# Linear attention with a routed expert layer: the first key group's maxima and exponentials unit by unit, its keys in three transfers, and one product on zeros less

## Chip, cores, metric

One core of a Trainium2 chip. The metric is the device time of one execution of the whole program in microseconds, as the median of several runs. A profiled execution gives the trace from which the rows below are taken.

## What is computed

```python
def phi(x):                                   # random-feature map, M = 128 features
    proj = einsum('bhsd,md->bhsm', x, omega)
    h = proj - sum(x * x, axis=-1, keepdims=True) / 2
    h = h - max(h, axis=-1, keepdims=True)
    return exp(h) / sqrt(m)
q_p, k_p = phi(q * scale), phi(k * scale)     # batch 4, heads 8, sequence 576, head size 64
kv = einsum('bhsm,bhsd->bhmd', k_p, v)
z = sum(k_p, axis=2)
attn = einsum('bhsm,bhmd->bhsd', q_p, kv) / (einsum('bhsm,bhm->bhs', q_p, z)[..., None] + 1e-6)
x = attn as [2304, 512]
# then: logits = x @ w_gate, each row goes to the expert of its largest logit (8 experts, capacity 576),
# out = gate weight * (relu(x @ w1[e]) @ w2[e])
```

## The kernel before

The kernel writes out the order of every engine's instructions by hand; what each engine waits for follows from the tiles that an instruction reads and writes. Its time falls into a key stage (to about 48 us), a query stage with the routing (to about 123 us) and the expert stage.

The keys come as 8 chunks (4 batches with 2 halves of the heads each), each 128 x 1152 numbers: 9 units of 128 columns. The loop over `n` takes the 72 units in 18 groups of `KG` = 4. Turn `n` does this:

- `project` (line 147): for each of the four units two products, `om_s` (the scaled features) with the upper and the lower 64 rows of the keys, into two banks `pjk`, four units side by side in each bank. Turns `n` and `n + 2` use the same two banks, so group 2's products overwrite what group 0 left. A product in this number format stands as two records (passes) in the trace, so a group has 16 passes.
- `kv_acc` (line 200): the sums of group `n - 2`, exponentials times values, 32 records, tile `kacc`.
- the maxima over 128 features (VectorE) and the exponentials (ScalarE) of group `n`. For the first bank, one reduction over all four units (line 153) and four exponentials with the negated maximum as bias (line 531); for the second bank, one reduction, one subtraction of the maximum over all four units on VectorE (line 534) and one exponential over all of it (line 535).

On TensorE the order is thus: products of groups 0, 1 and 2, sums of group 0, products of group 3, sums of group 1, and so on.

Ahead of the loop TensorE multiplies zeros (`warm`, line 244), `WARM` = 3 times, each as two passes. The first chunk's keys (`kraw`) come in pieces whose borders are `FIRST_CUTS`; with 0, 128, 384, 768, 1152 group 0 (units 0 to 3) needs the first three pieces, group 1 (units 4 to 7) the third and fourth, and group 2 unit 8 of the fourth and three units of the next chunk. All of these transfers are issued by SP, one after another, with the first values (`v`) behind the second piece.

Of the kernel before, what the change touches and what calls it, by code (L numbers as in the profile page):

```python
# [13 lines left out]
AF = mybir.ActivationFunctionType  # L14
ALU = mybir.AluOpType
AX = mybir.AxisListType
# [3 lines left out]
B, H, S, D, M = 4, 8, 576, 64, 128  # L20
# [2 lines left out]
NT = N // 128  # L23
ROW = 73
SLOTS = 576
FIRST_CUTS = [0, 128, 384, 768, 1152]
SUB = 128
NSUB = 5
REST = SLOTS - 4 * SUB
# [6 lines left out]
NJ = 11  # L36
EPS = 1e-6 * M
BIG = 1048576.0
WARM = 3

HI_AT = ({0: ((1, 2),), 1: ((1, 3),), 2: ((2, 0),), 3: ((2, 1),), 4: ((2, 2),), 5: ((2, 3),)}, {0: ((2, 0),), 1: ((2, 1),), 3: ((2, 2),), 4: ((2, 3),)})
LO_AT = ({0: ((1, 2),), 1: ((1, 3),), 3: ((2, 0),), 4: ((2, 1),), 5: ((2, 2),), 6: ((2, 3),)}, {1: ((2, 0),), 2: ((2, 1),), 5: ((2, 2),), 6: ((2, 3),)})
# [8 lines left out]
def attention_moe(ctx, tc, kT, qT, va, om, wg, w1, w2, cap, ident, tri, desc, lst, tab0, out):  # L51
    nc = tc.nc
# [12 lines left out]
    def bank(i, name):  # L65
        return ps.tile([128, 512], F32, tag=f"b{i}", name=name, bufs=1)

    def pair(name):
        return ps.tile([128, 1024], F32, tag="a2", name=name, bufs=1)
# [55 lines left out]
    def start(gen):  # L125
        tasks.append([gen, None])

    def run(at=None, times=1, most=99):
        for _ in range(times):
            for task in list(tasks):  # L130
                if task[1] is None or (task[1] == at and most > 0):
                    most -= task[1] is not None
                    try:
                        task[1] = next(task[0])
                    except StopIteration:
                        tasks.remove(task)
# [6 lines left out]
    def project(parts, banks):  # L143
        for k, x in enumerate(parts):
            for i in range(2):
                rows = slice(64 * i, 64 * i + 64)
                nc.tensor.matmul(banks[i][:, k * M : (k + 1) * M], x[rows, :], om_s[rows, :], start=True, stop=True)  # L147

    def units(x):
        return x.rearrange("p (a m) -> p a m", m=M)  # L150

    def maxima(mx, i, src):
        nc.vector.tensor_reduce(mx[:, 4 * i : 4 * i + 4], src, op=ALU.max, axis=AX.X, negate=True)  # L153

    def spread(mx, i):
        return mx[:, 4 * i : 4 * i + 4].unsqueeze(2).to_broadcast([128, 4, M])
# [6 lines left out]
    def load_q(c):  # L163
        n0, n1 = QB[c] * 128, QB[c + 1] * 128
        raw = qp.tile([128, NP, QT * 128], F32, tag="qraw", name=f"qraw{c}")
        nc.sync.dma_start(raw[:, :, 0 : n1 - n0], qT[:, :, n0:n1])
        qc[c] = raw
# [8 lines left out]
    def load_k(b, g):  # L176
# [3 lines left out]
        if b == 0 and g == 0:  # L180
            for i, (c0, c1) in enumerate(zip(FIRST_CUTS, FIRST_CUTS[1:])):
                nc.sync.dma_start(raw[:, c0:c1], kT[b, :, g * W + c0 : g * W + c1])
# [12 lines left out]
    def kv_acc(b, g, t, ex, k, acc):  # L195
        v = chunks[b, g][1]
        a, z, o = (t, t + 1, 0) if t < 4 else ((4, 6, 0) if t == 4 else (t + 1, t + 2, VW))
        for i in range(2):
            for f in (0, 64):
                nc.tensor.matmul(  # L200
                    acc[f : f + 64, i * 2 * VW + o : i * 2 * VW + o + (z - a) * VW],
                    ex[:, 4 * i + k, f : f + 64],
                    v[:, i, a * VW : z * VW],
                    start=(t == 0 and i == 0),
                    stop=(t == 8),
                    skip_group_check=True,
                )
# [34 lines left out]
    wps = bank(SM, "wps")  # L242
    for _ in range(WARM):
        nc.tensor.matmul(wps[:, 0:256], warm[:, 0:128], warm, start=True, stop=True)
# [209 lines left out]
    def numer(t, qpT, acc):  # L454
        for p in range(NP):
            for i in range(2):
                for r in (0, 64):
                    nc.tensor.matmul(  # L458
                        acc[r : r + 64, i * 512 + p * ROW : i * 512 + (p + 1) * ROW],
                        qpT[:, 4 * i + p, r : r + 64],  # L460
                        kv_sb[(t * 128 + r) // S][:, 2 * p + i, :],
                        start=(p == 0),
                        stop=(p == NP - 1),
                        skip_group_check=True,
                    )
# [23 lines left out]
    NK = len(KU) // KG  # L489
    ex_l, d_l, qT_l, acc_l = {}, {}, {}, {}  # L490

    for n in range(NK + NT + 3):
        kn, t = n, n - NK
        mx = small.tile([128, H], F32, tag="mx", name=f"mx{n}", bufs=4) if n < NK + NT else None

        if n < NK:
            pj = [bank(2 * (n % 2) + i, f"pjk{n}{i}") for i in range(2)]
            project([chunks[b, g][0][:, u * 128 : (u + 1) * 128] for b, g, u in KU[KG * n : KG * n + KG]], pj)
        elif t < NT:
            pj = [bank((2 * t + i) % 3, f"pjq{n}{i}") for i in range(2)]  # L500
            c = max(i for i in range(len(QB) - 1) if QB[i] <= t)
            o = (t - QB[c]) * 128
            project([qc[c][:, p, o : o + 128] for p in range(NP)], pj)
        run("T")

        if 0 <= t - 2 < NT:
            d = d_l.pop(t - 2)
            trs = [bank(3 + i, f"qtr{n}{i}") for i in range(2)]
            for u in range(H):
                nc.tensor.transpose(trs[u // 4][:, (u % 4) * M : (u % 4 + 1) * M], d[:, u, :], id_sb)  # L510
        run()

        if 0 <= n - 2 < NK:
            ex = ex_l.pop(n - 2)
            for k, (b, g, u) in enumerate(KU[KG * (n - 2) : KG * (n - 1)]):
                if u == 0:
                    acc_l[0] = bank(4, f"kacc{b}{g}") if g == 0 else pair(f"kacc{b}{g}")
                kv_acc(b, g, u, ex, k, acc_l[0])
                if u == 8:
                    start(kv_gate(b, g, acc_l[0]))  # L520
        elif 0 <= t - 3 < NT:
            acc_l[0] = pair(f"qacc{t}")
            numer(t - 3, qT_l.pop(t - 3), acc_l[0])
        run("N")

        if n < NK:
            ex = kp.tile([128, H, M], F32, tag="ex", name=f"ex{n}", bufs=3)
            maxima(mx, 0, units(pj[0]))
            run()
            for k in range(4):  # L530
                nc.scalar.activation(ex[:, k, :], pj[0][:, k * M : (k + 1) * M], AF.Exp, bias=mx[:, k : k + 1], scale=1.0)  # L531
            maxima(mx, 1, units(pj[1]))
            run()
            nc.vector.tensor_tensor(ex[:, 4:8, :], units(pj[1]), spread(mx, 1), op=ALU.add)
            nc.scalar.activation(ex[:, 4:8, :], ex[:, 4:8, :], AF.Exp)
            ex_l[n] = ex
            run()
        else:
            if t < NT:
                d = qp.tile([128, H, M], F32, tag="d", name=f"d{t}", bufs=3)  # L540
                nc.scalar.copy(d[:, 0:4, :], units(pj[0]))
                maxima(mx, 1, units(pj[1]))
                run()
                maxima(mx, 0, d[:, 0:4, :])
                nc.gpsimd.tensor_tensor(d[:, 0:4, :], d[:, 0:4, :], spread(mx, 0), op=ALU.add)  # L545
                d_l[t] = d
            run("P", times=2, most=2)
            if 0 <= t - 2 < NT:
                qpT = qp.tile([128, H, M], F32, tag="qpT", name=f"qpT{t}", bufs=2)
                for i in range(2):  # L550
                    nc.scalar.activation(qpT[:, 4 * i : 4 * i + 4, :], units(trs[i]), AF.Exp)
                qT_l[t - 2] = qpT
                run()
            if t < NT:
                for k in range(4):
                    nc.scalar.activation(
                        d[:, 4 + k, :], pj[1][:, k * M : (k + 1) * M], AF.Identity, bias=mx[:, 4 + k : 5 + k], scale=1.0
                    )
                run()
            if 0 <= t - 3 < NT:  # L560
                normalise(t - 3, acc_l[0])
                if t - 3 in GROUPS:
                    start(route(*GROUPS[t - 3]))
                if t == 3:
                    start(first_item())
            run(times=3)
        run("E")

        if n == NK + 1:
            kstack.close()  # L570
            open_experts()
        if n < NK:

            for k in range(KB, 2 * B):
                if (9 * (k - KB) + 8) // KG + 2 == n:
                    load_k(k // 2, k % 2)
            if n == 3:
                start(setup())
            if n in (NK - 4, NK - 2):
                load_q(0 if n == NK - 4 else 1)  # L580
        elif t < NT and t - QB[c] == 2 and c + 2 < len(QB) - 1:
            load_q(c + 2)
# [265 lines left out]
```

## Time and profile before

| | |
|---|---|
| median of 3 runs | 296.16 us (295.9 to 296.26) |
| the profiled execution's own time | 297.4 us |
| its span, first to last instruction | 295.3 us |
| TensorE busy | 277.4 us, 94% |
| VectorE busy | 162.8 us, 55% |
| ScalarE busy | 152.9 us, 52% |
| mean granted clock of TensorE | 0.978 |

Shares over the whole span hide that the stages have different limits; the change lies in the first ten microseconds, which are 3% of the span, and what they are worth is read from when TensorE's unbroken row of work begins. In the rows, PE is TensorE, PEld its weight loads, DVE VectorE, ACT ScalarE, POOL GpSimd, SP the engine that issues most transfers (SPq its queue). A time in a timeline is counted from the span's start.

### The profile page before, as it was taken

The numbers are of one execution on the slowest core, as the hardware profiler recorded it, in microseconds if no ns is written. First come the engines' busy times: TensorE is split into PE (matmuls) and PEld (weight loads), VectorE is DVE, ScalarE is ACT, GpSimd is POOL, SyncE is SP. The second block draws the span as 40 slices with busy tenths as digits, with TensorE's granted clock in tenths as the row PEclk, the third lists the DMA queues.
The fourth block names the chain that finished last, engine by engine and source line by source line (L and its number), as shares of the span: only waits on it lengthen the run. The fifth ranks groups of instructions, "written<-read, shape, count | busy, mean of one in ns | idle before, by whom it ended". The sixth has DMA issues, their size and how long they took to land.

```text
span 295.3 us, 7405 instructions
## 1 busy us (share of the span) xinstructions
PE 277.4 (94%) x2958; PEld 240.7 (81%) x2958; DVE 162.8 (55%) x357; ACT 152.9 (52%) x371; POOL 75.2 (25%) x78
## 2 busy tenths in 40 slices
PE   7999999999999969799999999999999999999960
PEld 5898898889988958799957879996888899868850
DVE  1998788578887896576834332543333152532220
ACT  1887788868888745155416324543541345342410
POOL 1000000422674315750718100700121162011120
PEclk9999999999999987999999999999999999999995
DMA  6989730328667702286029914910811097064010
GB/s 204 395 310 364 244 139 4 99 66 287 232 201 261 293 36 73 86 271 238 2 60 372 372 52 111 332 42 4 269 65 73 36 295 152 0 178 165 37 54 28
DMA packets 29504, 48.01 MB, mean 163 GB/s; under 512 B 4835, under 2 KB 17507, under 8 KB 29444
## 3 DMA queue, kind: packets, MB, share of 16 engines
q1 hardware_dynamic: 26900, 41.45, 41.9%
q0 software_dynamic: 2416, 5.92, 6.3%
q8 instruction: 25, 0.41, 0.6%
q14 instruction: 19, 0.16, 0.2%
q10 hardware_dynamic: 144, 0.07, 0.1%
HBM read 35.61 MB, written 12.10 MB: 162 GB/s over the span
## 4 chain that ended last, share of the span: by engine, by line
PE 88%; DVE 4%; issue 2%; DMA 1%; ACT 1%; SPq 0%; POOL 0%
PE hi L676 9%; PE hi L678 9%; PE hi L677 9%; PE qacc L458 7%; PE yi L693 7%; PE kacc L200 7%; PE yi L694 7%; PE yi L695 7%; PE pjq L147 6%; PE pjk L147 6%; PE qtr L510 5%; PE xtri L328 3%; DVE xr L475 1%; DMA kraw<-kT 1%; PE yi0r L705 1%
## 5 line engine op out<-in xcount | busy, mean ns | idle before, releaser
L676 PE MATMUL hi<-xhi,w1hi 128*128 128x288 f32 x192 | 57.0, 297 | 0.0
L678 PE MATMUL hi<-xlo,w1hi 128*128 128x288 f32 x192 | 56.6, 295 | 0.0
L677 PE MATMUL hi<-xhi,w1lo 128*128 128x288 f32 x192 | 56.5, 294 | 0.0
L681 ACT ACTIVATE hhii<-hi 128x288 fp32r<-128x288 f32 (+1 forms) x48 | 18.5, 385 | 46.6 <-PE hi L678 45.4
L545 POOL TENSOR_TENSOR d<-d,mx 128x512 f32<-128x512 f32 x18 | 18.7, 1038 | 86.1 <-DVE mx L153 79.6
L693 PE MATMUL yi<-w2hi,hhii 128*128 128x512 f32 x96 | 39.0, 406 | 0.0
L684 DVE SCALAR_TENSOR_TENSOR hloi<-hi,hhii 128x288 fp32r<-128x288 f32 (+1 forms) x48 | 20.3, 423 | 33.3 <-ACT hfi L683 21.8
L694 PE MATMUL yi<-w2hi,hloi 128*128 128x512 f32 x96 | 38.0, 396 | 0.0
L695 PE MATMUL yi<-w2lo,hhii 128*128 128x512 f32 x96 | 37.9, 395 | 0.0
L334 DVE TENSOR_TENSOR xlo<-xtri,xhi 128x512 fp32r<-128x512 f32 (+1 forms) x20 | 12.5, 635 | 45.5 <-ACT xhi L332 45.5
L676 PEld LDWEIGHTS hi<-xhi,w1hi 128*128 128x128 f32 x192 | 36.0, 188 | 0.2
L677 PEld LDWEIGHTS hi<-xhi,w1lo 128*128 128x128 f32 x192 | 36.0, 188 | 0.0
L678 PEld LDWEIGHTS hi<-xlo,w1hi 128*128 128x128 f32 x192 | 36.0, 188 | 0.0
L98 POOL DMA_INDIRECT out<-ysi,idx x10 | 9.8, 981 | 73.6 <-ACT ysi L727 45.1
L314 POOL DMA_INDIRECT xg<-x_d,idx x15 | 19.0, 1264 | 35.8 <-PE hi L678 22.4
L153 DVE TENSOR_REDUCE mx<-pjk 128x4 f32<-128x512 f32 x36 | 23.1, 684 | 6.4 <-PE pjk L147 6.1
L458 PE MATMUL qacc<-kv_sb,qpT 128*64 128x73 f32 x576 | 23.4, 235 | 2.6 <-DVE xr L475 2.6
L458 PEld LDWEIGHTS qacc<-kv_sb,qpT 128*64 128x64 f32 x576 | 20.8, 141 | 5.8 <-issue 4.0
L531 ACT ACTIVATE ex<-pjk,mx 128x128 f32<-128x128 f32 x72 | 20.5, 368 | 7.0 <-DVE mx L153 6.5
L98 POOL DMA_INDIRECT tab_d<-pay,slot x18 | 19.3, 1070 | 15.8 <-DVE slot L399 10.6
L147 PE MATMUL pjk<-om_s,kraw 64*128 64x128 f32 x288 | 22.1, 292 | 1.1 <-ACT ex L531 0.6
L200 PE MATMUL kacc<-v,ex 128*64 128x65 f32 (+1 forms) x576 | 22.6, 230 | 0.2 <-issue 0.2
(126 smaller groups left out, 472.9 us busy)
## 6 DMA issues: line engine op xcount, KB each, us to landing
w1raw<-w SPq DMA_DIRECT2D x16, 512.0 KB, 5.9
w2raw<-w SPq DMA_DIRECT2D x16, 512.0 KB, 6.4
qraw<-qT SPq DMA_DIRECT2D x6, 768.0 KB, 6.2
x_d<-xr SPq DMA_DIRECT2D x18, 256.0 KB, 2.9
v<-va SPq DMA_DIRECT2D x7, 650.0 KB, 7.5
kraw<-kT SPq DMA_DIRECT2D x7, 576.0 KB, 7.1
out<-zero_sb SPq DMA_DIRECT2D x4, 768.0 KB, 7.9
out<-ysi SPq DMA_DIRECT2D x4, 256.0 KB, 4.6
```

The lines of the kernel that those rows point to most:

```text
L98: ins = nc.gpsimd.indirect_dma_start(out=dst, out_offset=bass.IndirectOffsetOnAxis(ap=index, axis=0), in_=src, in_offset=None, bounds_chec ...
L147: nc.tensor.matmul(banks[i][:, k * M : (k + 1) * M], x[rows, :], om_s[rows, :], start=True, stop=True)
L153: nc.vector.tensor_reduce(mx[:, 4 * i : 4 * i + 4], src, op=ALU.max, axis=AX.X, negate=True)
L200: nc.tensor.matmul(acc[f : f + 64, i * 2 * VW + o : i * 2 * VW + o + (z - a) * VW], ex[:, 4 * i + k, f : f + 64], v[:, i, a * VW : z * VW] ...
L458: nc.tensor.matmul(acc[r : r + 64, i * 512 + p * ROW : i * 512 + (p + 1) * ROW], qpT[:, 4 * i + p, r : r + 64], kv_sb[(t * 128 + r) // S][ ...
L531: nc.scalar.activation(ex[:, k, :], pj[0][:, k * M : (k + 1) * M], AF.Exp, bias=mx[:, k : k + 1], scale=1.0)
L676: nc.tensor.matmul(pt, whi_[:, k, fs], xhi[:, k, sl], start=(k == 0), stop=False)
L677: nc.tensor.matmul(pt, wlo_[:, k, fs], xhi[:, k, sl], start=False, stop=False)
L678: nc.tensor.matmul(pt, whi_[:, k, fs], xlo[:, k, sl], start=False, stop=(k == 3))
L693: nc.tensor.matmul(pt, hhi[:, f, sl], w2hi, start=(f == 0), stop=False)
L694: nc.tensor.matmul(pt, hlo[:, f, sl], w2hi, start=False, stop=False)
L695: nc.tensor.matmul(pt, hhi[:, f, sl], w2lo, start=False, stop=(f == 7))
```

## The change

Three edits. `FIRST_CUTS` becomes 0, 128, 512, 1152: group 0 needs two pieces, group 1 the third alone. `WARM` becomes 2. In turn 0 alone, the maxima and exponentials go unit by unit, the two banks taking turns: for each unit one reduction over 128 columns and one exponential with its result as bias; the subtraction on VectorE and the exponential over 512 columns are gone for this group.

```diff
-FIRST_CUTS = [0, 128, 384, 768, 1152]
+FIRST_CUTS = [0, 128, 512, 1152]
...
-WARM = 3
+WARM = 2
...
         if n < NK:
             ex = kp.tile([128, H, M], F32, tag="ex", name=f"ex{n}", bufs=3)
+        if n == 0:
+
+            for k in range(4):
+                for i in range(2):
+                    u, src = 4 * i + k, pj[i][:, k * M : (k + 1) * M]
+                    nc.vector.tensor_reduce(mx[:, u : u + 1], src, op=ALU.max, axis=AX.X, negate=True)
+                    nc.scalar.activation(ex[:, u, :], src, AF.Exp, bias=mx[:, u : u + 1], scale=1.0)
+            ex_l[n] = ex
+        elif n < NK:
             maxima(mx, 0, units(pj[0]))
```

VectorE's queue from the scaling of the features on, before (`mx` holds the maxima, `pjk_133` and `pjk_134` are group 0's two banks, `pjk_153` and `pjk_154` group 1's; in brackets the semaphores that an instruction waits for):

```order
L250 TENSOR_SCALAR om_s<-om_sb 128x128 [waits DMAHW0_49]
L153 TENSOR_REDUCE mx_132<-pjk_133 128x4 [waits PE_49]
L153 TENSOR_REDUCE mx_132<-pjk_134 128x4 [waits PE_49]
L534 TENSOR_TENSOR ex_143<-pjk_134,mx_132 128x512 [waits DVE_49]
L153 TENSOR_REDUCE mx_152<-pjk_153 128x4 [waits PE_49]
```

The same place of the change, where the banks of group 0 are `pjk_131` and `pjk_132`:

```order
L250 TENSOR_SCALAR om_s<-om_sb 128x128 [waits DMAHW0_49]
L533 TENSOR_REDUCE mx_130<-pjk_131 128x1 [waits PE_49]
L533 TENSOR_REDUCE mx_130<-pjk_132 128x1 [waits PE_49]
L533 TENSOR_REDUCE mx_130<-pjk_131 128x1 [waits Activation_49]
L533 TENSOR_REDUCE mx_130<-pjk_132 128x1 [waits Activation_49]
L533 TENSOR_REDUCE mx_130<-pjk_131 128x1 [waits Activation_49]
L533 TENSOR_REDUCE mx_130<-pjk_132 128x1 [waits Activation_49]
L533 TENSOR_REDUCE mx_130<-pjk_131 128x1 [waits Activation_49]
L533 TENSOR_REDUCE mx_130<-pjk_132 128x1 [waits Activation_49]
L153 TENSOR_REDUCE mx_158<-pjk_159 128x4 [waits PE_49]
```

Three instructions have become eight, and from the third on each waits for ScalarE, namely for the exponential that read the same bank before it.

TensorE's queue around the first two groups, before (`kraw_100` is the first chunk, `kraw_113` the second):

```order
L147 MATMUL pjk_133<-om_s,kraw_100 128x128 [waits DMAHW1_49,DVE_49]
...
L147 MATMUL pjk_133<-om_s,kraw_100 128x128 [waits DMAHW2_49]
...
L147 MATMUL pjk_133<-om_s,kraw_100 128x128 [waits DMAHW4_49]
...
L147 MATMUL pjk_153<-om_s,kraw_100 128x128 [waits DMAHW5_49]
...
L147 MATMUL pjk_173<-om_s,kraw_100 128x128 [waits DVE_49,Activation_49]
L147 MATMUL pjk_174<-om_s,kraw_100 128x128 [waits DVE_49,PE_49]
L147 MATMUL pjk_173<-om_s,kraw_113 128x128 [waits DMAHW6_49]
```

And of the change, where the second chunk is `kraw_111`:

```order
L147 MATMUL pjk_131<-om_s,kraw_100 128x128 [waits DMAHW1_49,DVE_49]
...
L147 MATMUL pjk_131<-om_s,kraw_100 128x128 [waits DMAHW2_49]
...
L147 MATMUL pjk_159<-om_s,kraw_100 128x128 [waits DMAHW4_49]
...
L147 MATMUL pjk_179<-om_s,kraw_100 128x128 [waits Activation_49]
L147 MATMUL pjk_180<-om_s,kraw_100 128x128 [waits Activation_49]
L147 MATMUL pjk_179<-om_s,kraw_111 128x128 [waits DMAHW5_49]
```

The wait inside group 0 for a third piece is gone, group 1 waits once, ahead of its first unit, and group 2 waits for ScalarE alone to free both banks.

SP's queue loses one transfer and changes two (before with -, the change with +):

```order
 L182 DMA kraw_100<-kT 128x128
-L182 DMA kraw_100<-kT 128x256
+L182 DMA kraw_100<-kT 128x384
 L184 DMA v_101<-va 128x2x260
-L182 DMA kraw_100<-kT 128x384 x2
-L187 DMA kraw_113<-kT 128x1152
+L182 DMA kraw_100<-kT 128x640
+L187 DMA kraw_111<-kT 128x1152
 L185 DMA v_101<-va 128x2x390
```

The second chunk's keys and all later transfers move up by one issue.

## Rows read from the trace of the kernel before

**Rows 1.** Busy time by stretch: length, then each engine, granted clock, DMA share, GB/s:

```profile
0.00:8.47 8.47, 6.17 (x38) 4.48 (x38) 2.38 (x5) 2.42 (x5) 0.95 (x7) 1.00 0.73 223
8.47:50.00 41.53, 41.30 (x840) 36.90 (x840) 36.39 (x68) 34.05 (x98) 0.00 (x0) 1.00 0.69 250
```

**Rows 2.** What TensorE waited for, 8.4 to 50 us: total, times, longest:

```profile
PE pjk L147 <- ACT ex L531: 0.6, 1, 0.6
```

**Rows 3.** The chain that ended last: shares, then 0 to 13 us (start, length, what):

```profile
PE 88%; DVE 4%; issue 2%; DMA 1%; ACT 1%; SPq 0%; POOL 0%
...
2.15 3.84 DMA kraw<-kT
...
6.57 0.69 DVE mx L153
...
7.28 1.15 ACT ex L531 x4
...
8.47 1.37 PE pjk L147 x16
9.85 1.08 PE kacc L200 x32
```

**Rows 4.** Timeline of VectorE, 4 to 11 us: start, length, instructions:

```profile
6.55 1.29 DVE L153 TENSOR_REDUCE mx<-pjk 128x4 f32<-128x512 f32 x2 [3.43 <-PE pjk L147]
7.88 0.69 DVE L534 TENSOR_TENSOR ex<-pjk,mx 128x512 f32<-128x512 f32 x1
```

**Rows 5.** Timeline of TensorE, 0 to 12 us (second row: 1.7 to 2.6):

```profile
1.18 2.93 PE L244 MATMUL wps<-warm 128*128 128x256 f32 x6 [1.18 <-DVE warm L241]
...
1.18 1.65 PE L244 MATMUL wps<-warm 128*128 128x256 f32 x3 [1.18 <-DVE warm L241]
...
4.04 1.65 PE L147 MATMUL pjk<-om_s,kraw 64*128 64x128 f32 x12
6.03 0.94 PE L147 MATMUL pjk<-om_s,kraw 64*128 64x128 f32 x12 [0.34 <-DMA kraw<-kT]
...
10.86 1.16 PE L147 MATMUL pjk<-om_s,kraw 64*128 64x128 f32 x16
```

**Rows 6.** Timelines of SP's queue and of VectorE, 0 to 5 us:

```profile
0.73 0.90 SPq L182 DMA_DIRECT2D kraw<-kT  x2
...
2.15 0.94 SPq L182 DMA_DIRECT2D kraw<-kT  x2
3.13 0.43 SPq L187 DMA_DIRECT2D kraw<-kT  x1
...
2.90 0.23 DVE L250 TENSOR_SCALAR om_s<-om_sb 128x128 f32<-128x128 f32 x1 [1.77 <-DMA om_sb<-om]
```

**Rows 7.** us from issue to landing: second piece, fourth piece, second chunk:

```profile
kraw<-kT SPq DMA_DIRECT2D x1, 128.0 KB, 2.2
...
kraw<-kT SPq DMA_DIRECT2D x1, 192.0 KB, 4.4
...
kraw<-kT SPq DMA_DIRECT2D x1, 576.0 KB, 5.6
```

**Rows 8.** TensorE's timeline around 110 us, and that stretch as in rows 1:

```profile
108.92 0.24 PE L374 MATMUL posr<-cum,ones_b 128*128 128x96 bf16 x1 [2.43 <-DVE cum L362]
...
109.21 2.08 PE L147 MATMUL pjq<-om_s,qraw 64*128 64x128 f32 x16
...
113.11 2.19 PE L458 MATMUL qacc<-kv_sb,qpT 128*64 128x73 f32 x32
...
108.30:115.10 6.80, 6.17 (x58) 5.44 (x57) 5.73 (x20) 2.81 (x7) 2.37 (x3) 0.50 0.11 41
```

**Rows 9.** Prices by line and form: count, busy us, mean ns of one:

```profile
L153 DVE TENSOR_REDUCE mx<-pjk 128x4 f32<-128x512 f32 x36 | 23.1, 684 | 6.4 <-PE pjk L147 6.1
...
L348 DVE TENSOR_REDUCE mxr<-lg 128x12 f32<-128x96 f32 x1 | 0.3, 253 | 0.0
...
L531 ACT ACTIVATE ex<-pjk,mx 128x128 f32<-128x128 f32 x72 | 20.5, 368 | 7.0 <-DVE mx L153 6.5
```

## The prediction

> **What bounds the kernel now.** I read the table of stretches first, then the chain of work that ended last, then the timelines of the first 11 us, since all three edits lie there. The stretches show TensorE busy for 41.30 of 41.53 us from 8.47 to 50, while VectorE and ScalarE have 5 to 7 us to spare; ahead of 8.47 it is busy for 6.17 of 8.47 [rows 1]. From 8.4 to 50 us its list of waits has one of note, 0.6 us, which is the one that ends at 8.47 [rows 2]. So from 8.47 on the key stage is a row of products, and what happens ahead of it is worth what it moves that start. The later stages follow TensorE as well: 88% of the whole chain is its work [rows 3], and the waits on VectorE in it come behind products of the same stage and move with them.
>
> The chain says what sets that start: a piece of keys lands at 2.15 + 3.84 = 5.99, the last passes of group 0 follow, VectorE's first maxima from 6.57, ScalarE's four exponentials from 7.28 to 8.43, and at 8.47 group 2's products, which overwrite group 0's banks [rows 3]. VectorE leaves the second bank at 7.88 + 0.69 = 8.57 [rows 4]; group 0's sums (from 9.85) come only behind group 2's products. Three things therefore must happen earlier if the kernel is to gain: the two banks of group 0 must come free, the keys of group 2 must be there, and group 1's products must be done.
>
> **The end of the warm products.** Each product stands as two passes. The three on zeros run from 1.18 to 4.11, three passes end at 2.83 and six at 4.11, so a pass is (4.11 - 2.83) / 3 = 0.427 us [rows 5]. The first key product starts at 4.04, 0.07 before the last record ends. With four passes the records end at 4.11 - 0.85 = 3.26, and the first key product can start at 3.19. Its other inputs are there: om_s is written by 2.90 + 0.23 = 3.13, and the first two pieces of keys had landed by 1.2 + 2.2 = 3.4 in their old size (SP issues the two from 0.73 in 0.90 us) [rows 6, 7]. The second piece grows from 128 to 192 KB. That costs between nothing and 64 KB at the 223 GB/s of the stretch to 8.47, 0.29 us [rows 1]; I take the latter, 3.7. Unit 0's passes occupy TensorE from 3.19 for about 0.6 us, so unit 1 is not held.
>
> **Group 0's products.** In the old order two pieces (3.4 and 5.99) had to land before the fourth unit. Now all four units run at one go. Twelve such passes took 1.65 us from 4.04 and 0.94 from 6.03 [rows 5], so the start ran at the slower pace, and sixteen passes at that pace stand at 109.21, where the granted clock was 0.50: 2.08 us [rows 8]. They end at 3.19 + 2.08 = 5.27, and VectorE starts about 0.03 later, at 5.30, against 6.55 [rows 4]: **1.25 us earlier**.
>
> **Maxima and exponentials unit by unit.** What VectorE does is two reductions over 512 (1.29 us) and an addition (0.69); it becomes eight reductions over 128. No such reduction stands in the trace. It is bounded by 0.253 (over 96) and 0.684 (over 512), which differ by 1.04 ns an element, so 0.253 + 32 x 1.04 = 0.286 us [rows 9]. ScalarE's four small exponentials and one of 512 become eight small ones, 0.368 each [rows 9].
>
> They do not overlap freely. The order shows that from the third on each reduction waits for ScalarE: it is the exponential that read the same bank just before. So in one bank the two engines take turns. A turn is 0.286 + 0.02 to ScalarE (the maximum ends at 6.57 + 0.69 = 7.26, the exponential starts at 7.28) + 0.368 + 0.04 back (as from ScalarE's 8.43 to TensorE's 8.47) = 0.715 us [rows 3]. Four turns less the last way back are 2.83 us for the first bank. The second trails by the spacing of two exponentials, (1.15 - 0.368) / 3 = 0.26 us [rows 3]: 3.09. Before, the banks came free 8.43 - 6.55 = 1.88 and 7.88 + 0.69 - 6.55 = 2.02 us after the start. **The new way takes about 1.0 us longer**, and gives back most of the 1.25: 5.30 + 2.83 = 8.13 against 8.43, and 8.39 against 8.57. With 0.04 to TensorE, group 2 starts at 8.17 and its second bank at 8.43: **-0.2 us**.
>
> The Trainium skill bears on this ("PSUM — Partial Sum Buffer", section "PSUM bank collisions raise a hardware error"): two engines may not touch one bank in the same partitions at once, reads by ScalarE and VectorE included. If that were not so, eight exponentials spaced by 0.26 behind the first maximum would end at 5.30 + 0.31 + 7 x 0.26 + 0.37 = 7.80, by which the banks would no longer be what group 2 waits for. No run here shows the two reading one bank together; the waits in the order show that this program does not try.
>
> **Group 1.** It needs the third piece, 320 KB, where it needed two pieces of 192 that landed at 5.99 and, issued with 0.47 us of SP for each, at 2.62 + 4.4 = 7.0 [rows 3, 6, 7]. The bytes ahead are the same, so I bound the landing by these two and take 6.9. Sixteen passes at full pace took 1.16 us [rows 5], with the last one starting some 0.27 before the end: TensorE is free for group 2 at 7.8 (at the late bound 8.0), still ahead of 8.17. VectorE is through with group 0 about 0.4 ahead of ScalarE, near 8.0, and takes up group 1 then; nothing waits for that.
>
> **Group 2's keys.** Its units 1 to 3 come from the next load, issued at 3.13 and landed 5.6 us later, 8.7 [rows 6, 7]. That is already within 0.2 us of being what holds group 2. One issue fewer moves it up by at most 0.47; if the engines' bytes alone set it, by nothing. With no move group 2 gains 0.03; with 0.2 or more it gains the full 0.2. I take **-0.15 us**. Later loads each wait for an older transfer, now one place earlier in the list; TensorE waited for none of them [rows 2].
>
> **Sum.** The profiled execution's own time is 297.4 us, 2.1 over its span of 295.3; the median of the plain runs is 296.16. -0.15 on either gives a span of 295.15 and a median of **296.0 us**. A measurement of this kernel can tell about 0.2%, 0.6 us, from no change, so this counts as no change.
>
> **Rivals.**
>
> *The clock comes later (slower).* By the two rows of twelve passes TensorE went from the lower level, 1.2 GHz, to 2.4 GHz between 5.7 and 6.3 us, although the granted clock is listed as 1.00 from the start [rows 1, 5]. Ahead of that it had worked from 1.18 with one pause of 0.34 us. Now it stops at about 5.1 and waits for the third piece until 6.9. If it stays at the lower level, group 1 takes 2.08 instead of 1.16, so group 2 starts at about 8.8, not 8.2, +0.35 on the 8.47 of before; if the clock stays low through group 2 and group 0's sums as well (2.08 instead of 1.16, and twice 1.08 [rows 3, 5, 8]), +0.35 + 0.92 + 1.08 = +2.35. Middle: +1.3, 297.5. For it speaks that at 109.21 work went on for some 6 us at 0.50 after a pause of 2.43 us [rows 8]; against it that ahead of 5.1 TensorE would have worked nearly 4 us with hardly a break. It decides when the clock is still low at 8.2. The page "TensorE: Matmul & The Clock Gate", section "What's actually happening", of the Trainium skill has the throttled state as the default, which activity releases; the trace agrees as far as these rows go, and by it an idle stretch moved into the start-up is a risk. Chance 0.26, of which two thirds pass 0.6 us.
>
> *The turns cost more.* If each hand-over took 0.1 more, seven of them move group 2 by +0.7 - 0.2 = +0.5: 296.7. The rows give 0.02 to 0.05 everywhere, so 0.06.
>
> *The turns cost less and the keys come with the issue (faster).* With 0.2 for a reduction and 0.3 for an exponential a turn is 0.56 and the banks are free at 7.8; keys at 8.7 - 0.47 = 8.2 leave -0.5 to -0.6: 295.6. Chance 0.12.
>
> *The pause in the middle falls elsewhere (faster).* At 108.3 the clock fell to 0.50, after TensorE had waited from 106.5 for VectorE's routing, and came back at 115.1; the work from 109.21 to 113.11 + 2.19 = 115.30 took 6.1 us, half of it for the halved clock [rows 8]. Any move of the work can change how much of it falls into the slow stretch; half of those 3 us saved would be -1.5: 294.6. Nothing in the rows says that 0.15 us suffices: 0.12.
>
> **How the numbers follow.** No change of note is left with 0.44, its own range 295.6 to 296.6. Faster by over 0.6 us: the middle pause 0.12, nearly half of the quick turns, and some of the main case's edge: 0.20. Slower: two thirds of the late clock, half of the costly turns, a little edge: 0.25. The rest, 0.55, is within 0.2%. The range of 294.9 to 297.4 leaves a tenth on each side.
>
> **What would show it.** Group 0's first maximum at 5.3 +-0.15, the last exponential of the turns ending at 8.4, group 2's first product at 8.2, and group 1's sixteen passes in 1.16 us. I am wrong if these still take 2.08, if group 2 starts later than 8.5, or if the stretch of low clock behind 105 us is of another length.

## The result and the profile after

The changed kernel is slower: 298.09 us (median of 6 runs, 297.73 to 298.46) against 296.21 (295.67 to 297.27), a ratio of 1.0061 [1.0042, 1.008], +1.9 us where 296.0 was forecast. Its profiled execution took 298.25 us over a span of 296.1.

Busy time by stretch of the changed kernel (columns as in [rows 1]):

```profile
0.00:8.47 8.47, 5.08 (x32) 3.76 (x34) 2.64 (x10) 3.55 (x9) 0.95 (x7) 1.00 0.76 250
8.47:50.00 41.53, 41.16 (x816) 36.83 (x816) 34.91 (x65) 32.30 (x94) 0.00 (x0) 0.96 0.68 244
5.60:7.70 2.10, 0.00 (x0) 0.00 (x0) 1.56 (x6) 1.60 (x6) 0.00 (x0) 1.00 0.98 331
9.10:12.50 3.40, 3.40 (x47) 3.12 (x44) 3.33 (x6) 2.65 (x9) 0.00 (x0) 0.50 1.04 403
12.50:50.00 37.50, 37.13 (x766) 33.13 (x764) 31.42 (x60) 29.42 (x85) 0.00 (x0) 1.00 0.65 227
```

Against [rows 1], TensorE's granted clock from 8.47 to 50 is no longer 1.00 but 0.96, and it does 24 records fewer in that stretch (816, not 840) though it is busy nearly all of it. The whole loss of clock lies between 9.1 and 12.5, at 0.50, which is the lower of its two levels, 1.2 GHz. Ahead of it stands a stretch of 2.1 us with no work of TensorE at all, while the DMA engines are busy for 0.98 of the time.

TensorE's timeline of the changed kernel, 0 to 14 us (the products split by group):

```profile
1.19 2.07 PE L244 MATMUL wps<-warm 128*128 128x256 f32 x4 [1.19 <-DVE warm L241]
3.20 2.35 PE L147 MATMUL pjk<-om_s,kraw 64*128 64x128 f32 x16
7.75 1.16 PE L147 MATMUL pjk<-om_s,kraw 64*128 64x128 f32 x16 [2.20 <-DMA kraw<-kT]
8.74 2.06 PE L147 MATMUL pjk<-om_s,kraw 64*128 64x128 f32 x16
10.74 1.96 PE L200 MATMUL kacc<-v,ex 128*64 128x65 f32 x32
12.62 1.16 PE L147 MATMUL pjk<-om_s,kraw 64*128 64x128 f32 x16
```

Group 0's sums in the same view of the kernel before:

```profile
9.77 1.15 PE L200 MATMUL kacc<-v,ex 128*64 128x65 f32 x32
```

Group 0 starts 0.84 earlier than before, as meant. Then TensorE waits 2.20 us for the third piece of keys. Group 1 runs at full pace (16 passes in 1.16); group 2 begins at 8.74, 0.27 later than before; its products take 2.00 to the next row's start and group 0's sums 1.88, where before they took 9.77 - 8.47 = 1.30 and 10.86 - 9.77 = 1.09 [rows 3, 5]. Group 3 begins at 12.62, not 10.86: 0.27 + 0.70 + 0.79 = **1.76 us late**, of which 1.49 is the halved clock.

VectorE's and ScalarE's timelines, then the groups by line and form, of the changed kernel:

```profile
5.58 0.49 DVE L533 TENSOR_REDUCE mx<-pjk 128x1 f32<-128x128 f32 x2 [2.45 <-PE pjk L147]
...
6.30 0.55 DVE L533 TENSOR_REDUCE mx<-pjk 128x1 f32<-128x128 f32 x2 [0.23 <-ACT ex L534]
...
5.90 2.80 ACT L534 ACTIVATE ex<-pjk,mx 128x128 f32<-128x128 f32 x8 [3.45 <-DVE mx L533]
...
L533 DVE TENSOR_REDUCE mx<-pjk 128x1 f32<-128x128 f32 x8 | 2.1, 290 | 3.0 <-PE pjk L147 2.4 <-ACT ex L534 0.6
...
L534 ACT ACTIVATE ex<-pjk,mx 128x128 f32<-128x128 f32 x8 | 2.5, 364 | 3.8 <-DVE mx L533 3.5
```

The turns begin at 5.58, and their last exponential ends at 5.90 + 2.80 = 8.70.

Where the 1.76 go later, the timeline of the changed kernel from 108 us and the middle stretch of low clock:

```profile
110.60 0.20 PE L374 MATMUL posr<-cum,ones_b 128*128 128x96 bf16 x1 [2.43 <-DVE cum L362]
...
123.60 0.40 PE L685 MATMUL hi<-xhi,w1hi 128*128 128x288 f32 x1
...
111.50:114.90 3.40, 3.40 (x30) 2.85 (x28) 3.30 (x12) 1.80 (x4) 0.64 (x1) 0.50 0.22 82
```

The first expert product in the trace of before:

```profile
123.14 0.40 PE L676 MATMUL hi<-xhi,w1hi 128*128 128x288 f32 x1
```

The routing's product stands at 110.60, not 108.92 [rows 8]: 1.68 later, so the start's loss has come through the whole key stage. The clock falls here for 3.4 us, not 6.8, and from this product to the first expert product it is 13.00 us; in the trace of before that product stands at 123.14, 14.22 behind. So the two profiled spans differ by only 0.8 us. That is because the one of before was 297.4, 1.2 over its own median; the plain runs give the change's price.

### The profile page after: what moved, and what is told of

Its sections match the earlier page's. It is cut to its first block, busy times and chain, and to the rows that moved or that the text cites. A ratio compares the mean times of both kernels' runs of the same rounds, so it can differ in the third digit from the quotient of the medians.

```text
span 296.1 us, 7406 instructions
## 1 busy us (share of the span) xinstructions
PE 276.7 (93%) x2956; PEld 240.2 (81%) x2956; DVE 162.7 (55%) x362; ACT 153.6 (52%) x374; POOL 76.4 (26%) x78
## 5 line engine op out<-in xcount | busy, mean ns | idle before, releaser
L334 DVE TENSOR_TENSOR xlo<-xtri,xhi 128x512 fp32r<-128x512 f32 (+1 forms) x20 | 12.5, 634 | 45.5 <-ACT xhi L332 45.5
L314 POOL DMA_INDIRECT xg<-x_d,idx x15 | 19.7, 1313 | 36.5 <-DMA idx<-tab_d 26.4
L458 PE MATMUL qacc<-kv_sb,qpT 128*64 128x73 f32 x576 | 22.8, 231 | 2.6 <-DVE xr L475 2.6
L147 PE MATMUL pjk<-om_s,kraw 64*128 64x128 f32 x288 | 22.8, 301 | 2.2 <-DMA kraw<-kT 2.2
L458 PEld LDWEIGHTS qacc<-kv_sb,qpT 128*64 128x64 f32 x576 | 20.2, 138 | 5.8 <-issue 4.0
L153 DVE TENSOR_REDUCE mx<-pjk 128x4 f32<-128x512 f32 x34 | 21.9, 684 | 4.8 <-PE pjk L147 4.4
L147 PEld LDWEIGHTS pjk<-om_s,kraw 64*128 64x128 f32 x288 | 19.1, 200 | 4.6 <-DMA kraw<-kT 2.7
```

The source lines that it names most:

```text
L458: nc.tensor.matmul(acc[r : r + 64, i * 512 + p * ROW : i * 512 + (p + 1) * ROW], qpT[:, 4 * i + p, r : r + 64], kv_sb[(t * 128 + r) // S][ ...
```

## Experiments

All ratios are to the kernel before, run beside it on the same chip, with a 95% interval; 12 runs each (4 in one case, 11 in another). They are not the quotients of the medians, and where the two differ the text says which it uses. "Filling" means products on zeros into a bank that nobody reads, behind group 0's products; "mid filling" is the same during the routing's wait at 106.5 us. Each kernel does all the work of the reference.

### Is it the clock, the keys or the turns?

Filling the pause with four products (the kernel is otherwise the changed one):

```diff
         project(...)
+        if n == 0:
+            for _ in range(4):
+                nc.tensor.matmul(wps[:, 0:256], warm[:, 0:128], warm, start=True, stop=True)
```

> The changed kernel with four more products on zeros behind group 0's products, where TensorE waits for the third piece of keys (5.5 to 7.75 us). Clock theory (the pause makes the clock fall at about 9 us, and group 2's products and group 0's sums then run at half pace): the clock stays up, group 3's products start near 10.9 instead of 12.62, and the time is 296.2 +-0.5, about 1.9 below the changed kernel. Keys or turns theory (the late third piece or the alternation of maxima and exponentials delays the work itself): the fill changes nothing, 298.1, or costs a little more.

297.35 us, 1.0031 [1.0011, 1.0051]. TensorE's timeline from 5.3 us, and the stretch that was low:

```profile
5.35 2.42 PE L501 MATMUL wps<-warm 128*128 128x256 f32 x8
7.70 2.34 PE L147 MATMUL pjk<-om_s,kraw 64*128 64x128 f32 x32
9.97 1.15 PE L200 MATMUL kacc<-v,ex 128*64 128x65 f32 x32
11.05 1.16 PE L147 MATMUL pjk<-om_s,kraw 64*128 64x128 f32 x16
...
9.10:12.50 3.40, 3.40 (x67) 3.09 (x68) 3.33 (x6) 2.70 (x9) 0.00 (x0) 1.00 1.03 400
```

The piece still lands at about 7.7 and the turns are as before, but the clock holds at 1.00, 67 records fit where there were 47, and group 3 begins at 11.05, 0.19 behind the kernel before. So of the 1.76, 1.57 hang on the pause in this pair of traces. The runs won back only half of the 0.61%, 0.30 +-0.28 by the two intervals, for a reason that this trace does not show in the start; it has the long low stretch (6.8 us) in the middle.

The three edits undone one at a time:

```diff
+WARM = 3                                 # e2
...
+FIRST_CUTS = [0, 128, 384, 768, 1152]    # e3
...
-        if n == 0:
+        if n == -1:                       # e4: the old maxima
```

> The changed kernel with the third warm product put back. Clock theory: group 0's products end 0.85 us later, near 6.4, the pause shrinks from 2.2 to about 1.4 us, and most of the loss goes: 296.2 to 297. Keys or turns theory: the later start of group 0 only adds, 298.1 to 298.9.

298.15 us, 1.0049 [1.0024, 1.0075]. TensorE's timeline, 8 to 11 us:

```profile
8.80 2.33 PE L147 MATMUL pjk<-om_s,kraw 64*128 64x128 f32 x16 [1.12 <-ACT ex L534]
```

The piece was there at 6.52, and the pause moved behind group 1: 1.12 us for the turns' exponentials, again followed by half pace; group 3 at 12.67. Not every execution pays: three of the 12 took 295.93 to 296.11 us, at a mean granted clock of 0.983 to 0.984, the other nine 297.64 to 299.55, eight of them at 0.976 to 0.978.

> The changed kernel with the old pieces of keys (borders 128, 384, 768). Clock theory: TensorE works again at 6 us, when the third piece lands, no pause is over 1 us, and the time is that of before, 296.2 +-0.5. Keys theory: 296.2 as well. Turns theory: the alternation starts at 6.6 and holds group 2 until 9.5, 297.2 to 298.

299.22 us (4 runs), 1.0108 [1.0094, 1.0123], the slowest of all. TensorE's timeline, 9 to 16 us:

```profile
9.36 2.33 PE L147 MATMUL pjk<-om_s,kraw 64*128 64x128 f32 x16 [1.25 <-ACT ex L534]
11.62 2.00 PE L200 MATMUL kacc<-v,ex 128*64 128x65 f32 x32
13.55 2.08 PE L147 MATMUL pjk<-om_s,kraw 64*128 64x128 f32 x16
```

Without the new cuts the wait for the turns is 1.25 us, and TensorE, which had not yet been at full pace, stays at half pace past group 3. Beside the new maxima the new cuts were the part that helped, not the part that hurt (1.0042 to 1.008 with them, 1.0094 to 1.0123 without); the theory that the 320 KB piece is the cause falls.

> The changed kernel with group 0's maxima and exponentials in the old way (one reduction for each bank); cuts and warm products as changed. Clock theory: the pause is the same, 298.1 +-0.4. Turns theory: the banks come free 1 us earlier, 296.5 to 297. Keys theory: 298.1.

296.67 us, 1.0015 [0.9991, 1.0039]: with the old maxima alone back, no loss is seen. TensorE's one pause of note in the start is 0.76 us (for the second piece); in this trace too it works at half pace until about 10.3, and group 3 begins at 11.71. I had held that the pause for the third piece would stay and cost as much, and that fell. In this execution the third piece was there when group 1 came to it, so the trace does not show the old maxima beside a late piece; that they cost no more than 0.39% over before is seen in the 12 runs.

### The same with the middle held

On this chip every kernel, that of before too (310.83), took some 14 us more. In the traces it lies in waits of TensorE behind 116 us, the longest for VectorE; ratios on one chip are hardly touched by that.

```diff
         pos_b = bank(SM, ...)
+        if a == 0:
+            for _ in range(5):
+                nc.tensor.matmul(pos_b[:, 256:512], warm[:, 0:128], warm, start=True, stop=True)
```

These three lines alone, in the kernel before:

> The kernel before with five products on zeros ahead of the routing's first product, into columns of its bank that nobody reads, so that TensorE works through the pause from 106.3 to 108.9 us. Clock theory: the clock doesn't fall there, the 6 us of work at half pace take 3, and the time falls by 1.5 to 3 us to 293.5 to 295, with less spread between runs. If the low clock in the middle costs nothing (the routing's chain on VectorE sets the pace there): 296.5, no change.

310.25 us, 0.9981 [0.995, 1.0012]; no fall of the clock at 108, group 3 at 11.12; the gain of 1.5 to 3 us is not there. The same lines in the changed kernel:

> The changed kernel with the same filling in the middle. What is left between this and the kernel before with the filling is the start alone. Clock theory and turns theory: 1.5 to 2 us slower than that kernel. If the changed kernel's loss came from another fall in the middle, the two would be equal within 0.3.

311.28 us, 1.0002 [0.9977, 1.0026]; a wait of 2.13 us for the third piece, low clock from 8.3 to 11.7, group 3 at 12.19. That kernel with the four filling products of the first experiment as well:

> The changed kernel with the filling in the middle and four products on zeros behind group 0. Clock theory: the start costs no half pace, so at most 0.3 over the kernel before with the filling in the middle, and 1.3 or more under the changed one with it. Turns theory: the alternation still holds group 2, so the time is that of the changed kernel with the filling.

310.52 us, 0.9997 [0.9973, 1.0021]; group 3 at 11.26. And the kernel before with the mid filling and, of the change, the new maxima alone:

```diff
+        if n == 0:
+            for k in range(4):
+                for i in range(2):
...
-            maxima(mx, 0, units(pj[0]))
+        elif n < NK:
+            maxima(mx, 0, units(pj[0]))
```

> The kernel before with the filling in the middle and, of the change, the unit-by-unit maxima and exponentials alone (old cuts, three warm products). Turns theory: group 2 starts 1.0 us later than before (9.5) and the wait of 1.6 us makes the clock fall besides: 1 to 3 us slower than the kernel before with the filling. Keys theory: equal to it.

311.88 us, 1.0024 [0.999, 1.0058]. By the medians, against the first of the four the changed kernel is 1.0 us slower, the filled one 0.3, and the maxima alone 1.6; by the ratios the differences are 0.21, 0.16 and 0.43%. The order is that of the first experiments, but the intervals overlap, and by the ratios the filling wins only 0.05% here, where 1.3 us was expected; this supports and does not show. TensorE's timeline of the new maxima alone, 8 to 14 us:

```profile
9.40 1.41 PE L147 MATMUL pjk<-om_s,kraw 64*128 64x128 f32 x16 [1.59 <-ACT ex L537]
```

With three warm products and the old pieces the new maxima by themselves make a pause of 1.59 us; the clock is low from 10.7 to 14.1.

### The other two edits alone, and the middle by itself

```diff
-FIRST_CUTS = [0, 128, 384, 768, 1152]
+FIRST_CUTS = [0, 128, 512, 1152]          # f1, before otherwise
...
-WARM = 3
+WARM = 2                                  # f2, before otherwise
```

> The kernel before with the new cuts alone (old maxima, three warm products). If the pauses of TensorE behind group 0 decide: group 0 ends at 6.1 instead of 6.5, group 1 waits for its one piece until 6.4 to 7.7, no pause over 1.6 us, 296.2 to 297.2. If the larger third piece itself costs: 297.5 or more.

296.63 us, 0.9985 [0.996, 1.001], group 3 at 10.31.

> The kernel before with two warm products instead of three, nothing else. Group 0 still waits for its third piece until 6.0, so the 0.85 us taken away opens a pause between 4.9 and 6.0. If such a pause alone keeps the clock low or lets it fall: 297 to 298.5. If only the wait for the banks in the unit-by-unit way does the harm: 296.2 +-0.4.

297.70 us, 1.0025 [1.0, 1.0051], group 3 at 11.58. TensorE's timeline, 5 to 9.5 us:

```profile
5.34 3.75 PE L147 MATMUL pjk<-om_s,kraw 64*128 64x128 f32 x24 [0.32 <-DMA kraw<-kT]
```

24 passes take 3.75 us where 12 took 0.94 in [rows 5]: with a warm product less, half pace lasts to about 9 in this trace. The cuts tend to help and the missing product tends to cost; neither is told from nothing for certain.

The kernel before with the mid filling alone (the diff above), on a chip without the 14 us:

> The kernel before with five products on zeros in the routing's pause, as once already on a chip where everything took 14 us longer behind the routing and the effect in the middle could not be read from the time. Clock theory: no fall at 108 us, 1.2 to 2.7 us faster than the kernel before.

297.37 us, 1.0008 [0.9983, 1.0032]: the gain is not there. Its windows:

```profile
9.50:12.80 3.30, 3.30 (x44) 3.08 (x44) 2.31 (x5) 2.13 (x8) 0.00 (x0) 0.50 1.04 406
108.00:115.00 7.00, 6.82 (x77) 5.75 (x77) 6.76 (x22) 4.02 (x12) 1.86 (x2) 1.00 0.12 44
```

The middle held its clock, and nothing was gained there: VectorE is busy for 6.76 of the 7 us, and TensorE then waits for it. The first row shows something else: this kernel's start is that of before, and in this execution its clock fell at 9.5, behind pauses of 0.50, 0.29 and 0.56 us; group 3 began at 12.95. What the start costs therefore differs from execution to execution, and the kernel before pays it in some too.

The changed kernel with the old maxima, two filling products and the mid filling:

```diff
-        if n == 0:
+        if n == -1:
...
+        if n == 0:
+            for _ in range(2):
+                nc.tensor.matmul(wps[:, 0:256], warm[:, 0:128], warm, start=True, stop=True)
...
+        if a == 0:
+            for _ in range(5):
+                nc.tensor.matmul(pos_b[:, 256:512], warm[:, 0:128], warm, start=True, stop=True)
```

> New cuts, old maxima, two products on zeros ahead of group 0 and two behind it, and the filling in the routing's pause. Group 0's maxima start at 5.3 and its banks are free at about 7.4, so group 2 starts right behind group 1, at 7.6 to 8.6. Clock theory: 0.2 to 0.8 us under the kernel before with the filling in the middle alone, 1.5 to 3 under the kernel before. Rival: the filled products run at half pace and hold up group 1, equal to the filling in the middle alone or slower by up to 0.5.

296.71 us, 1.0002 [0.9984, 1.0021]; group 3 at 10.72, and no fall of the clock in the start or in the middle. Even so the median is that of before.

### The change again, and versions that might beat both

This chip is again one with the 14 us (before: 310.41). The changed kernel a second time, with no edit:

> The changed kernel itself, beside the three that follow, on the same chip, with a second trace. Clock theory: TensorE is again without work for about 2 us in all between group 0's and group 2's products, group 3's products start 1 to 2 us later than the 10.86 of before, and the time is 0.4 to 0.8% over before. If its first trace caught a rare case, group 3 starts near 11 and the time is within 0.2%.

312.14 us, 1.0043 [1.0016, 1.0071]: the loss is there again. TensorE's timeline of this second trace, 5 to 12 us:

```profile
6.24 4.33 PE L147 MATMUL pjk<-om_s,kraw 64*128 64x128 f32 x32 [0.74 <-DMA kraw<-kT]
10.50 1.15 PE L200 MATMUL kacc<-v,ex 128*64 128x65 f32 x32
11.58 1.16 PE L147 MATMUL pjk<-om_s,kraw 64*128 64x128 f32 x16
```

Here the third piece was there at 6.24, and yet 32 passes took 4.26 us to the next row's start: the clock rose only at about 10.2. This is the late rise that the rival described; the first trace of the same kernel had full pace from 7.75 and a fall at 9.1. Of the two signs expected, neither came: the pause is 0.74 us, not about 2, and group 3 at 11.58 is only 0.72 behind the 10.86 of before. That is less than half of the 1.7 us by which the medians differ; where the rest arose is not shown, as the kernel before has no trace on this chip.

The other three edit the start once more: the changed kernel with the old maxima and four filling products, the changed kernel with two, and the kernel before with the new cuts and one:

```diff
+            for _ in range(4):               # g2, and the old maxima
+            for _ in range(2):               # g3
+            for _ in range(1):               # g4, and of the change FIRST_CUTS alone
                 nc.tensor.matmul(wps[:, 0:256], warm[:, 0:128], warm, start=True, stop=True)
```

> New cuts, two warm products, four products on zeros behind group 0, and the old maxima and exponentials: the filled changed kernel without the unit-by-unit part. If, once the pause is filled, the alternation of reduction and exponential costs by itself: 0.3 to 1 us under the filled changed kernel (which had 0.31% over before), so 0 to 0.2% over before. If only the pause counts: the same 0.3% over before.

311.01 us, 1.0006 [0.9979, 1.0033]; group 3 at 10.89.

> The changed kernel with two products on zeros behind group 0 instead of four, 0.85 us at full and 1.7 at half pace. Clock theory, with four being too long where they run at half pace: between the unfilled changed kernel and before, 0.1 to 0.4% over before. If filling does nothing: 0.6%.

310.52 us, 1.0007 [0.9984, 1.003]. The time equals that of before, though in its own trace full pace came late, at about 10.5, and group 3 began at 12.19. That trace is of the slowest of the 12 runs, 312.29 us, so it does not stand for the median; it shows that filling does not bring the clock up in every execution.

> The new cuts alone (three warm products, old maxima) and one product on zeros behind group 0, in the pause of 0.8 us ahead of group 1. Clock theory: no pause of note is left ahead of the third group, 0.1 to 0.4% under before. Otherwise equal to the cuts alone, -0.15 +-0.25%.

309.99 us, 0.9982 [0.9955, 1.001]; group 3 at 10.63. This is the lowest ratio of the four measured together, as that of the cuts alone was of its four. Both beat the changed kernel; neither is separated from the one before.

## Why the prediction was wrong

**The step that failed** is "-0.15": that group 2's start follows from the banks and the keys alone, with TensorE at full pace from 5.7 us on. Group 2 did not come earlier but 0.27 later, and the clock, at full pace as it began, was halved from 9.1 to 12.5. The 0.27 are two mis-sized terms, the third piece (7.65 for 6.9), which held group 1 and behind it group 2, and group 0's products (2.35 for 2.08), which started the turns later; the 1.49 are the rival "the clock comes later", which had the right side and, between its middle of "+1.3" and its end of "+2.35", the size, but a chance of 0.26 and another course. It was to be a late rise; in the first trace it is a fall after a pause, in the second the late rise.

Point by point:

- *Warm products end 0.85 earlier*: right (3.26; first key product at 3.20, said 3.19).
- *Group 0's 16 passes in 2.08, VectorE at 5.30*: 2.35 and 5.58. The second piece, 192 KB, was taken at 3.7 and held its unit to 3.89; the rest is half pace as said.
- *Turns*: right. 0.290 and 0.364 us were measured for 0.286 and 0.368, and 3.12 from the first maximum to the last exponential for 3.09. "About 1.0 us longer" than the old way held as well: 3.12 against 2.02. The Trainium skill ("PSUM — Partial Sum Buffer", section "PSUM bank collisions raise a hardware error") forbids two engines one bank in the same partitions at once. The trace agrees: the third reduction, on the first bank, begins at 6.30, behind that bank's first exponential, which ended at 5.90 + 0.36 = 6.26.
- *Third piece at 6.9*: it landed at 7.65 (issue at 2.15 and 5.5 us). In the traces of other executions TensorE began on it at 6.52 and 6.24, so the bounds of 5.99 and 7.0 were too narrow on one side only.
- *Group 1 in 1.16*: right in the trace shown; in the second trace of the same kernel it was half pace.
- *Group 2 at 8.2, its second bank at 8.43*: 8.74, straight behind group 1. The turns freed the second bank at 8.70, and the first, one spacing of exponentials (0.26) sooner, at about 8.44; without the late piece group 2 could have begun there.
- *The pause in the middle*: its length did change, 3.4 for 6.8 us, which the text had named as a sign of being wrong. Its price was mis-sized: half of "those 3 us" was taken as 1.5. Measured, the long stretch costs 14.22 - 13.00 = 1.22 over the short one, and no fall at all gains nothing more: in two traces without it (the missing warm product alone, and the old maxima with both fillings) that way is 12.99 and 13.00 us, because TensorE then waits for VectorE. In the first of them that wait is 1.92 us, where in the trace of before it is 0.38:

```profile
109.41 0.20 PE L374 MATMUL posr<-cum,ones_b 128*128 128x96 bf16 x1 [2.42 <-DVE cum L362]
115.96 1.25 PE L458 MATMUL qacc<-kv_sb,qpT 128*64 128x73 f32 x32 [1.92 <-DVE xr L475]
122.40 0.40 PE L676 MATMUL hi<-xhi,w1hi 128*128 128x288 f32 x1
```

**What stands in its place.** Group 2 cannot begin before about 8.4 or use its second bank before 8.7, since the turns take a microsecond longer than the old maxima; where the third piece is late, as in the trace shown first, it holds group 1 and so group 2 to the same point. Everything that was made earlier ahead of that point (a warm product less, group 0 at one go) could then only become idle time of TensorE: in the traces with the new maxima and no filling its pauses between 3.2 us and group 2 were 2.20, 2.13, 0.68 + 1.12, 0.59 + 1.25, 1.59 and 0.74. In each, part of the work behind, to between 10 and 16 us, went at half pace.

Half pace alone does not tell the new maxima from the old, though, since three traces with the old ones have it too (11.71, 11.58 and 12.95 for group 3). All 18 traces, sorted by the durations of the passes, say more. In five full pace came only behind 9 us; all five have two warm products (of 11 such traces), none of the seven with three. In the other 13 it was there by 8.2 us, and what counts is whether it fell again before 14: with the new maxima and nothing filled behind group 0 in four of four, with the old maxima and nothing filled in one of four, with filling in none of five. These are few traces, so they support the two ways in which the clock was lost and do not give their share.

The page "TensorE: Matmul & The Clock Gate" (section "What's actually happening") of the Trainium skill has the low clock as the state without activity; the trace agrees, with 0.50 from 9.1 behind the pause of 2.20, and 1.00 where it was filled.

Which edit it is, the ratios tell, in pairs of kernels that differ in the maxima alone (the +- of a difference is worked out from the two intervals, taken as independent):

| beside the maxima | new | old | difference |
|---|---|---|---|
| new cuts, two warm products | +0.61%, again +0.43% | +0.15% | 0.46 +-0.31, again 0.28 +-0.36 |
| new cuts, three warm products | +0.49% | -0.15% | 0.64 +-0.36 |
| old cuts, two warm products | +1.08% (4 runs) | +0.25% | 0.83 +-0.29 |
| old cuts, three, mid filling | +0.24% | -0.19% | 0.43 +-0.46 |

The new maxima are the dearer in every pair. In the second and third the intervals of the two ratios do not meet, nor do they in the first (1.0042 to 1.008, 0.9991 to 1.0039), though the second measurement of the changed kernel (1.0016 to 1.0071) overlaps with the old maxima there. So that the maxima cost is shown. That the clock is the way in which they cost is shown in the trace of the filled pause and goes with the tally of the traces; that it is all of it is not, since filling took off 0.30, 0.05 and 0.36% (each +-0.28 to 0.36) where it was tried on the new maxima. Left open: what the old maxima gain where the third piece is late (in the trace shown first the turns hold group 2 hardly longer than group 1 does), why the clock turns at other times in executions of one kernel, and how much the one missing warm product costs by itself. The first trace stands apart in this: its pause of 2.20 us is for the piece, and would be there with the old maxima too; no trace here has that pause with them and without filling.

## What to carry to other kernels

Making a first step earlier is worth nothing when the next holder (here banks in which two engines take turns, and a transfer in flight) does not move; it turns into idle time, and idle time of TensorE in a start-up can cost the clock for the next microseconds, far more than was to be won (here 1.49 us against 0.15). Before warm products are taken out or reductions split finer, add up TensorE's pauses from the first product to the first point that cannot move, and test the change with the pause filled. Splitting work between two engines by pieces of one bank makes a chain of turns (0.29 + 0.36 us and two hand-overs a piece); one reduction for a whole bank, with the other bank given to the other engine, freed both a microsecond sooner (2.02 us from the first maximum against 3.12).

## What the runs showed of the hardware

- The granted clock is listed as 1.00 ahead of its first recorded change, whatever the pace: in the kernel with the old cuts 16 passes took 2.08 us at 13.55, where full pace is 1.16, in a stretch listed at 1.00. Pace is read from durations there.
- One kernel's clock rose and fell at different times in different executions: the changed one was at full pace from 7.75 and low from 9.1 in one trace, and low throughout to 10.2 in another.
- Chips differ: on two of them every kernel, that of before too, took 14 us more. In the traces it lies in waits behind 116 us, not always at the same one; the longest is one for VectorE (10.92 us, where the same product waits 1.39 on another chip), and what held VectorE is not shown:

```profile
132.18 2.21 PE L461 MATMUL qacc<-kv_sb,qpT 128*64 128x73 f32 x32 [10.92 <-DVE xr L478]
```
